# Squaring before clamping in the first activation of an attention and two-MoE kernel

## The chip, the cores and the metric

The kernel runs on one core of a Trainium2 chip. The metric is the device time of one execution in microseconds. Before the change three runs gave 772.76, 773.0 and 776.55 us, a median of 773.0 us.

## The reference

Three stages follow one another over 2304 tokens. The first is attention over a window of 64 keys (4 sequences of 576 tokens, 8 heads of 64). The second is a dense feed-forward layer whose activation is the one changed here:

```python
h = x @ w_in                       # 512 -> 2048
neg, pos = h <= -1, h >= 1
g = np.where(pos, h, np.where(neg, 0.0, (h + 1) ** 2 / 4))
x = g @ w_out                      # 2048 -> 512
```

The third is a mixture of 8 experts, one expert per token, chosen by the largest of 8 gate logits:

```python
idx = argmax(x @ w_gate, axis=1)
out[t] = gate_w[t] * (relu(x[t] @ w1[idx[t]]) @ w2[idx[t]])
```

The inputs are float32. The activation can be written in two ways. For h at most 1, r^2 is at most 1 and max(h, 1) is 1, so both give r^2. For h above 1 the parabola lies above the line h, so both give h.

## The kernel before, in words

Every float32 operand of a matmul is split into a rounded high part and a low part, and a product is made of three passes (high by high, low by high, high by low), all in fp32r.

Tokens are cut into seven blocks of 256 or 384 columns (`BLOCKS`). The second stage goes through steps, one for each block and each of 16 slices of 128 hidden units, 112 steps in all. In a step, `layer1` (L440) makes `h`, 128 hidden units by 256 or 384 tokens, in one of two PSUM buffers with 12 matmuls. `act_g` (L447 to L458) turns `h` into `g`, again in a high and a low part (`ghi`, `glo`). `layer2` (L475) multiplies `g` with `w_out` and adds into `acc`. The main loop issues layer 1 of step i and then layer 2 of step i - 2, so a step's activation has some two steps of matmuls to get done. Layer 1 of step i + 2 needs the PSUM buffer that the activation of step i reads.

`act_g` is a chain over two engines. ScalarE makes `a` = Relu(0.5 h + 0.5) (L449). VectorE clamps it to 1 (L450). ScalarE squares it (L451). VectorE takes the maximum with `h` (L452), which is the last read of `h`. ScalarE rounds the result to `ghi` (L455), and VectorE, or GpSimd for six of the first steps (`GLO_P`), makes `glo` by subtraction (L456). The third stage has a shorter chain, `act_relu` (L464 on ScalarE, L465 on VectorE).

Other work is laid between these steps by slots, two per step. Attention units for later blocks bring score matmuls, a row maximum on VectorE (L336 or L354), exponentials on ScalarE (L364), transposes on TensorE (L399), a copy of them to SBUF as `pb` on ScalarE (L401) and the product with the values (L414). Weight pieces of the second stage are split on ScalarE, VectorE and GpSimd (L180 to L206). From the last block on, VectorE computes the gate logits, one instruction for each of 18 tiles of 128 tokens and each of 8 experts (L569, 144 in all). One expert's weights are then loaded and split (L642 on ScalarE, L643 on GpSimd), and tokens are turned into columns (L160, L910 on ScalarE, L911 on GpSimd). Tokens that didn't choose this expert are gathered at the end.

The order of instructions on each engine isn't the program's order. The program is built under a context that schedules by a simulated timeline, and only the first eight steps have the order of the DMA queue SP written out. So an instruction can run earlier than the place where the program issues it.

```python
with _tile.TileContext(nc, schedule_with_timeline_sim=True) as tc:
    tile_window_attention__then__two_moe_kernel(tc, *args)
```

Of the kernel before, what the change touches and what calls it, by code (L numbers as in the profile page):

```python
# [16 lines left out]
ALU = mybir.AluOpType  # L17
# [93 lines left out]
def kernel(  # L111
# [14 lines left out]
    nc = tc.nc  # L126
# [320 lines left out]
    def act_g(h, n, pool):  # L447
        a = gp.tile([P, NG], F32, tag="a", name="a", bufs=2)
        nc.scalar.activation(a[:, :n], h[:, :n], ACTF.Relu, scale=0.5, bias=half[:, 0:1])  # L449
        nc.vector.tensor_scalar(out=a[:, :n], in0=a[:, :n], scalar1=1.0, scalar2=None, op0=ALU.min)  # L450
        nc.scalar.activation(a[:, :n], a[:, :n], ACTF.Square)  # L451
        nc.vector.tensor_tensor(out=a[:, :n], in0=h[:, :n], in1=a[:, :n], op=ALU.max)  # L452
        hi = gp.tile([P, NG], F32R, tag="ghi", name="ghi")
        lo = gp.tile([P, NG], F32R, tag="glo", name="glo")
        nc.scalar.activation(hi[:, :n], a[:, :n], ACTF.Copy)  # L455
        (nc.gpsimd if pool else nc.vector).tensor_tensor(  # L456
            out=lo[:, :n], in0=a[:, :n], in1=hi[:, :n].bitcast(F32), op=ALU.subtract
        )  # L458
        return hi, lo
# [530 lines left out]
    for i in range(len(steps) + 2):  # L990
        if i == SPN:
            sp_order.close()
        if i < len(steps):
            ph, b, f = steps[i][:3]
            if ph == 1:
                n = blocks[b][1]
                while f not in win:
                    wsplit()
                g[i] = act_g(layer1(xT[b], win[f], n), n, i in GLO_P)
            else:  # L1000
                g[i] = act_relu(layer1(xT2[b], W2["p"][0][f], NG), NG)
        run_slot(base + 2 * i)
        wsplit(base + 2 * i)
        if i >= 2:
            ph, b, f, first, last, partial = steps[i - 2]
            n = blocks[b][1] if ph == 1 else NG
# [93 lines left out]
```

## Time and profile before

| what | value |
|---|---|
| median of three runs | 773.0 us |
| profiled execution | 774.57 us |
| its span | 772.8 us |
| TensorE busy | 727.8 us (94%) |
| VectorE busy | 519.5 us (67%) |
| ScalarE busy | 417.3 us (54%) |
| GpSimd busy | 207.3 us (27%) |

The profile is taken from one execution. Its span reaches from the first to the last instruction; 1.8 us of the execution lie around it. PE is TensorE, DVE is VectorE, ACT is ScalarE, POOL is GpSimd. PEclk is the granted clock of TensorE as a share of 2.4 GHz, so 0.50 stands for 1.2 GHz. A wait is the time that an engine stood idle ahead of an instruction, put down to what released it last.

### The profile page before, as it was taken

The page shows a single profiled execution, that of the slowest core. Times are in us where ns is not written, and L with a number is a line of the kernel's source. Part 1 is how long each engine was busy: PE and PEld are TensorE (multiplying, and loading weights), DVE is VectorE, ACT ScalarE, POOL GpSimd, SP SyncE. Part 2 cuts the span into 40 slices and gives each one's busy share as a digit, 9 for nine tenths or more (in the row PEclk, how much of TensorE's full clock was granted, in tenths as well). Part 3 has the DMA queues.
Part 4 walks back from the last instruction along what each step waited for, and adds up shares of the span by engine and source line. Part 5 has one row for each costly group of instructions (what it writes and reads, how often), then busy time and mean ns, then how long its engine had stood idle before and what let it go on. Part 6 is the DMA issues. An engine that isn't in the chain of part 4 may idle for free. (4 is left out here: it accounts for less than half of the span.)

```text
span 772.8 us, 12584 instructions
## 1 busy us (share of the span) xinstructions
PE 727.8 (94%) x4507; PEld 635.4 (82%) x4507; DVE 519.5 (67%) x1163; ACT 417.3 (54%) x1031; POOL 207.3 (27%) x164
## 2 busy tenths in 40 slices
PE   6698999999999999999999999979999999899996
PEld 3587878888888899888988898768988988799885
DVE  5887988548777668865797398999979854111110
ACT  4777766576656767575677444555533335441212
POOL 2466643204421024300320001561220116520000
PEclk7599999999999999999999999999999999999999
DMA  8446830143432324532343314432353134510101
GB/s 322 158 144 211 281 117 27 56 143 102 146 108 91 117 62 121 152 90 76 82 157 83 149 28 136 145 115 55 127 86 99 33 99 121 155 35 14 42 1 52
DMA packets 66691, 83.78 MB, mean 108 GB/s; under 512 B 35671, under 2 KB 41559, under 8 KB 66498
## 3 DMA queue, kind: packets, MB, share of 16 engines
q1 hardware_dynamic: 66466, 82.52, 34.6%
q8 instruction: 36, 0.59, 0.3%
q0 software_dynamic: 160, 0.43, 0.2%
q14 instruction: 29, 0.24, 0.1%
HBM read 60.74 MB, written 14.42 MB: 97 GB/s over the span
## 5 line engine op out<-in xcount | busy, mean ns | idle before, releaser
L440 PE MATMUL h<-xT,wi 128*128 128x384 f32 (+1 forms) x1344 | 233.5, 322 | 15.8 <-DVE a L452 12.8
L440 PEld LDWEIGHTS h<-xT,wi 128*128 128x128 f32 x1344 | 211.4, 193 | 30.3 <-DVE a L452 21.3
L475 PE MATMUL acc<-wo,ghi 128*128 128x512 f32 x576 | 155.7, 398 | 0.3 <-ACT ghi L455 0.2
L475 PEld LDWEIGHTS acc<-wo,ghi 128*128 128x128 f32 x576 | 104.3, 190 | 16.7 <-ACT ghi L455 1.0
L569 DVE CUSTOM_DVE_ANT_0 junk<-xg,wgb 128x512 bf16<-128x512 f32 x144 | 113.9, 791 | 2.4 <-DMA xg<-x2s 0.6
L440 PE MATMUL h<-xT,we 128*128 128x384 f32 x576 | 110.9, 337 | 3.2 <-DVE glo L465 3.2
L440 PEld LDWEIGHTS h<-xT,we 128*128 128x128 f32 x576 | 102.0, 188 | 9.0 <-DVE glo L465 4.7
L465 DVE SCALAR_TENSOR_TENSOR glo<-h,ghi 128x384 fp32r<-128x384 f32 x48 | 26.6, 554 | 93.2 <-ACT ghi L464 93.2
L475 PE MATMUL acc<-wo,glo 128*128 128x512 f32 x288 | 85.9, 395 | 0.6 <-DVE glo L456 0.5
L475 PE MATMUL acc<-we,ghi 128*128 128x512 f32 x288 | 79.3, 395 | 2.3 <-ACT ghi L464 2.2
L451 ACT ACTIVATE a<-a 128x384 f32<-128x384 f32 (+1 forms) x112 | 53.0, 474 | 50.6 <-DVE a L450 50.3
L456 DVE TENSOR_TENSOR glo<-a,ghi 128x384 fp32r<-128x384 f32 (+1 forms) x106 | 64.8, 612 | 21.4 <-ACT ghi L455 20.6
L455 ACT ACTIVATE ghi<-a 128x384 fp32r<-128x384 f32 (+1 forms) x112 | 53.0, 475 | 42.9 <-DVE a L452 42.0
L449 ACT ACTIVATE a<-h,half 128x384 f32<-128x384 f32 (+1 forms) x112 | 58.8, 525 | 30.5 <-PE h L440 29.1
L452 DVE TENSOR_TENSOR a<-h,a 128x384 f32<-128x384 f32 (+1 forms) x112 | 55.5, 497 | 26.1 <-ACT a L451 25.1
L450 DVE TENSOR_SCALAR a<-a 128x384 f32<-128x384 f32 (+1 forms) x112 | 48.9, 437 | 26.3 <-ACT a L449 26.1
L475 PEld LDWEIGHTS acc<-wo,glo 128*128 128x128 f32 x288 | 53.2, 188 | 13.5 <-DVE glo L456 1.9
L464 ACT ACTIVATE ghi<-h 128x384 fp32r<-128x384 f32 x48 | 23.1, 484 | 75.6 <-PE h L440 63.1
L475 PEld LDWEIGHTS acc<-we,ghi 128*128 128x128 f32 x288 | 52.8, 188 | 10.9 <-ACT ghi L464 2.4
L264 POOL TENSOR_TENSOR qs<-qk,qs 64x512 fp32r<-64x512 f32 x16 | 21.8, 1364 | 132.7 <-ACT qs L257 99.7
L911 POOL TENSOR_TENSOR xT<-xj,xT 128x256 fp32r<-128x256 f32 x36 | 30.5, 855 | 86.8 <-ACT xT L910 86.8
L643 POOL TENSOR_TENSOR we<-er,we 128x512 fp32r<-128x512 f32 x16 | 24.1, 1515 | 95.3 <-ACT we L642 95.3
(170 smaller groups left out, 979.8 us busy)
## 6 DMA issues: line engine op xcount, KB each, us to landing
qk<-in_qk_dram SPq DMA_DIRECT2D x21, 640.0 KB, 3.9
vt<-in_vv_dram SPq DMA_DIRECT2D x32, 256.0 KB, 2.8
er<-in_w_dram SPq DMA_DIRECT2D x32, 256.0 KB, 2.9
wraw<-in_wi_dram SPq DMA_DIRECT2D x14, 512.0 KB, 4.5
wraw<-in_wo_dram SPq DMA_DIRECT2D x14, 512.0 KB, 6.0
xg<-x2s SPq DMA_DIRECT2D x18, 256.0 KB, 2.7
out_dram<-y SPq DMA_DIRECT2D x18, 256.0 KB, 2.3
qk<-in_qq_dram SPq DMA_DIRECT2D x11, 320.0 KB, 3.2
```

Source lines behind the costliest of these rows:

```text
L440: nc.tensor.matmul(h[:, :n], w[:, wa, k * P:k * P + P], x[:, xa, k, :n], start=(i == 0), stop=(i == 3 * KD - 1),)
L449: nc.scalar.activation(a[:, :n], h[:, :n], ACTF.Relu, scale=0.5, bias=half[:, 0:1])
L450: nc.vector.tensor_scalar(out=a[:, :n], in0=a[:, :n], scalar1=1.0, scalar2=None, op0=ALU.min)
L451: nc.scalar.activation(a[:, :n], a[:, :n], ACTF.Square)
L452: nc.vector.tensor_tensor(out=a[:, :n], in0=h[:, :n], in1=a[:, :n], op=ALU.max)
L455: nc.scalar.activation(hi[:, :n], a[:, :n], ACTF.Copy)
L456: (nc.gpsimd if pool else nc.vector).tensor_tensor(out=lo[:, :n], in0=a[:, :n], in1=hi[:, :n].bitcast(F32), op=ALU.subtract)
L465: nc.vector.scalar_tensor_tensor(out=lo[:, :n], in0=h[:, :n], scalar=0.0, in1=hi[:, :n].bitcast(F32), op0=ALU.max, op1=ALU.subtract,)
L475: nc.tensor.matmul(a, ga[:, t * P:t * P + P], w[:, wa], start=(first and j == 0), stop=(last and j == 2),)
L569: nc.vector.tensor_tensor_reduce(out=junk, in0=xg[t], in1=Z["wgb"][:, e], scale=1.0, scalar=0.0, op0=ALU.mult, op1=ALU.add, accum_out=Z["L ...
L643: nc.gpsimd.tensor_tensor(out=w[:, 1], in0=raw, in1=w[:, 0].bitcast(F32), op=ALU.subtract)
L911: (nc.vector if 2 * t + i in PL_V else nc.gpsimd).tensor_tensor(out=lo, in0=r, in1=hi.bitcast(F32), op=ALU.subtract)
```

## The change

The clamp of L450 is gone. ScalarE does Relu and Square one after the other. One VectorE instruction then computes max(h, 1) and takes the minimum of that and the square, in a single pass with two operations.

```diff
     def act_g(h, n, pool):
         a = gp.tile([P, NG], F32, tag="a", name="a", bufs=2)
         nc.scalar.activation(a[:, :n], h[:, :n], ACTF.Relu, scale=0.5, bias=half[:, 0:1])
-        nc.vector.tensor_scalar(out=a[:, :n], in0=a[:, :n], scalar1=1.0, scalar2=None, op0=ALU.min)
         nc.scalar.activation(a[:, :n], a[:, :n], ACTF.Square)
-        nc.vector.tensor_tensor(out=a[:, :n], in0=h[:, :n], in1=a[:, :n], op=ALU.max)
+
+        nc.vector.scalar_tensor_tensor(
+            out=a[:, :n], in0=h[:, :n], scalar=1.0, in1=a[:, :n], op0=ALU.max, op1=ALU.min
+        )
```

## Rows read from the trace of the kernel before

**Rows 1.** The page's first part: busy us, share of the span, instructions.
```profile
PE 727.8 (94%) x4507; PEld 635.4 (82%) x4507; DVE 519.5 (67%) x1163; ACT 417.3 (54%) x1031; POOL 207.3 (27%) x164
```

**Rows 2.** Waits of PE, 80:478 then 478:546: total us, times, longest.
```profile
PE h L440 <- DVE a L452: 4.0, 9, 0.8
...
PE h L440 <- DVE a L452: 8.8, 5, 4.1
```

**Rows 3.** Busy us of PE, PEld, DVE, ACT, POOL by stretch; clock; DMA share; GB/s.
```profile
80.00:478.00 398.00, 391.01 (x2530) 343.42 (x2523) 294.86 (x619) 248.61 (x634) 91.78 (x59) 1.00 0.36 110
478.00:546.00 68.00, 59.18 (x277) 52.14 (x276) 66.95 (x156) 38.07 (x75) 31.62 (x24) 0.95 0.36 106
```

**Rows 4.** Groups of VectorE by form: busy us, mean ns, idle before, releaser.
```profile
L452 DVE TENSOR_TENSOR a<-h,a 128x384 f32<-128x384 f32 x64 | 35.3, 554 | 12.5 <-ACT a L451 12.1
...
L465 DVE SCALAR_TENSOR_TENSOR glo<-h,ghi 128x384 fp32r<-128x384 f32 x48 | 26.6, 554 | 93.2 <-ACT ghi L464 93.2
```

**Rows 5.** Tile `a`: ns min/median/max, first and last start; who waited for it.
```profile
L450 DVE TENSOR_SCALAR a<-a x112: 266/350/1698, 40.1 to 540.9; 128x384 f32<-128x384 f32 x64, 128x256 f32<-128x256 f32 x48
...
L452 DVE TENSOR_TENSOR a<-h,a x112: 393/546/559, 41.5 to 543.1; 128x384 f32<-128x384 f32 x64, 128x256 f32<-128x256 f32 x48
...
  ACT a L451: 50.3, 57
```

**Rows 6.** Timeline of ScalarE: start us, us, instruction, [idle before it <- releaser].
```profile
438.93 0.53 ACT L451 ACTIVATE a<-a 128x384 f32<-128x384 f32 x1 [0.43 <-DVE a L450]
...
505.28 0.79 ACT L160 ACTIVATE xj<-tt 128x512 uint16<-128x512 uint16 x1 [2.20 <-DVE glo L456]
506.11 0.42 ACT L910 ACTIVATE xT<-xj 128x256 fp32r<-128x256 f32 x1
```

**Rows 7.** Timeline of TensorE around 63 us.
```profile
62.16 0.66 PE L399 MATMUL pt<-ct,sr 128*128 128x128 f32 x4
64.88 1.46 PE L414 MATMUL av<-pb,vt 128*64 128x64 f32 x16 [2.07 <-ACT pb L401]
```

**Rows 8.** Timeline of ScalarE around 64 us.
```profile
63.92 0.42 ACT L451 ACTIVATE a<-a 128x256 f32<-128x256 f32 x1 [1.86 <-DVE a L450]
64.25 0.58 ACT L401 ACTIVATE pb<-pt 128x512 f32<-128x512 f32 x1
```

**Rows 9.** The stretch behind that wait, columns as in rows 3.
```profile
65.10:68.40 3.30, 3.30 (x23) 2.99 (x22) 2.04 (x5) 3.23 (x14) 2.42 (x2) 0.50 0.54 174
```

**Rows 10.** Timeline of VectorE around 178 us.
```profile
177.45 1.37 DVE L450 TENSOR_SCALAR a<-a 128x256 f32<-128x256 f32 x1
179.30 0.43 DVE L452 TENSOR_TENSOR a<-h,a 128x256 f32<-128x256 f32 x1 [0.48 <-ACT a L451]
```

**Rows 11.** Timeline of TensorE at 180 us.
```profile
179.78 1.70 PE L440 MATMUL h<-xT,wi 128*128 128x256 f32 x12 [0.49 <-DVE a L452]
```

**Rows 12.** Busy us of L450 alone, then of L569 alone; clock; DMA; GB/s.
```profile
479.00:523.00 44.00, 4.06 (x8) 0.96 0.42 124
...
478.00:546.00 68.00, 45.95 (x99) 0.95 0.36 106
```

**Rows 13.** Timeline of VectorE: the first gate logit, and one at 520 us.
```profile
444.80 0.69 DVE L569 CUSTOM_DVE_ANT_0 junk<-xg,wgb 128x512 bf16<-128x512 f32 x1 [0.58 <-DMA xg<-x2s]
...
519.75 1.75 DVE L569 CUSTOM_DVE_ANT_0 junk<-xg,wgb 128x512 bf16<-128x512 f32 x1
```

**Rows 14.** Timeline of TensorE in the last block.
```profile
464.91 2.35 PE L440 MATMUL h<-xT,wi 128*128 128x384 f32 x12
...
497.70 2.38 PE L440 MATMUL h<-xT,wi 128*128 128x384 f32 x12 [1.57 <-DVE a L452]
...
508.41 3.89 PE L440 MATMUL h<-xT,wi 128*128 128x384 f32 x12 [2.05 <-DVE a L452]
...
522.77 3.76 PE L440 MATMUL h<-xT,wi 128*128 128x384 f32 x12 [4.06 <-DVE a L452]
```

**Rows 15.** Timeline of GpSimd at 520 us.
```profile
519.58 1.38 POOL L643 TENSOR_TENSOR we<-er,we 128x512 fp32r<-128x512 f32 x1
```

## Prediction

> **What bounds the kernel now.** I read the page's first part, then the waits of TensorE, then the table of stretches, then the timelines around the waits it names. The page gives TensorE 727.8 of 772.8 us and VectorE 519.5 [rows 1]: matmuls are the bound and VectorE has room on average. An average hides the stages, so TensorE's waits are asked for by stage. From 80 to 478 us, where attention and the first layers run interleaved, it waits nine times for L452, 4.0 us in all; from 478 to 546 us five times, 8.8 us in all [rows 2]. L452 is the last reader of `h`, and `h` has two PSUM buffers, so layer 1 two steps later can't start before it. The two stages differ: in the first VectorE is busy 294.86 of 398 us, in the second 66.95 of 68 [rows 3]. In the first L452 is late because of latency and queueing, in the second because VectorE itself is the bound. There its work is the gate logits of L569, 45.95 us of the 68 [rows 12].
>
> **What the change removes.** The 112 VectorE instructions of L450, with a median of 350 ns and up to 1698 ns [rows 5]. And two crossings between engines: ScalarE waited 57 times, 50.3 us, for L450 before its Square [rows 5]. Where nothing queues that wait is 0.43 us [rows 6]. Afterwards Square follows Relu on the same engine. How soon a dependent ScalarE instruction starts is seen at 505.28 plus 0.79, which ends at 506.07; the one that reads its output starts at 506.11 [rows 6], so 0.04 us. An undisturbed chain gains 0.43 - 0.04 = 0.4 us.
>
> **What it adds.** L452 becomes a scalar_tensor_tensor with the same inputs, `h` in PSUM and `a`. Its nearest row is L465, the same form with a PSUM and an SBUF input: 554 ns at 384 columns, and the old L452 takes 554 too [rows 4]. I take no difference. Bounds: 350 ns below (L450's median, if it ran like that form), and above 554 + 350 = 904, both old instructions in one; even that would be no more VectorE time than now. It waits for Square, and what stands behind it on VectorE (mask adds, the row maxima, the weight splitting, gate logits) waits too. Before, that queue waited in two pieces, for Relu and for Square; now in one.
>
> What a change of order does I can't see. The code asks for scheduling by a simulated timeline, and the trace shows the reach of that: the first gate logit runs at 444.80 [rows 13], while the program issues it behind the first layer-1 group of the last block, which TensorE reaches at 464.91 [rows 14]. So a freed place on VectorE can be refilled with a gate logit from later. All three terms below carry this doubt.
>
> **Term A, the wait at 62.8 us.** The transposes end at 62.16 + 0.66 = 62.82, and the next matmuls start at 64.88 after 2.07 us of waiting for `pb` [rows 7]. ScalarE made `pb` late: it stood 1.86 us at Square, waiting for L450, and only then did the `pb` copy at 64.25, 0.58 us [rows 8]. Without L450 ScalarE is free by 62.5, the copy starts when the transposes end, about 62.85, and ends at 63.43; TensorE starts about 63.5. That is 64.88 - 63.48 = 1.4 us; what is late next is the copy itself. Right behind this wait the granted clock is 0.50, the 1.2 GHz level, for 3.3 us [rows 9]. The price of such a stretch is seen at 508.41: twelve matmuls take 3.89 us, at 497.70 the same twelve take 2.38 [rows 14], so 1.5 us. The wait of 1.57 us at 497.70 was followed by no such fall, so I count it as gone. A = 2.9 us; bounds 0 and 3.6 (2.07 + 1.5).
>
> **Term C, the nine waits from 80 to 478 us.** The one at 179.78 [rows 11] is typical of those that go whole: L450 took 1.37 us where its median is 0.35, and ended at 178.82, Square followed, L452 started at 179.30 [rows 10]. With Square done long before, the one VectorE instruction starts at 177.45 and ends before 178. Where L452 stands behind other VectorE work, only L450's own place, 0.35 us, comes back. The nine make 4.0 us; bounds 0 and 4.0. I take 2.4, six tenths.
>
> **Term E, VectorE bound from 478 to 546 us.** Between 479 and 523 us eight L450 take 4.06 us [rows 12], and the waits grow to 1.57, 2.05 and 4.06 us [rows 14]. If nothing refills the places, the last of these comes 4.1 us sooner. If gate logits refill them all, only the shorter chain is left, 0.4 to 0.7 us, since `h` comes free that much earlier once. I take 2.0, near the middle. Two of these waits are followed by matmuls at half the clock, 508.41 and 522.77 [rows 14]; I leave both as they are, and keep 2 x 1.5 us as a bound.
>
> **Sum.** 2.9 + 2.4 + 2.0 = 7.3 us. New waits from a new order I take at nothing, with 3.6 us (the largest wait of this kind and its half clock, as in A) either way. The profiled execution took 774.57 us (span 772.8 and 1.8 around it), so 767.3 for it. The median of the runs, 773.0, lies 1.6 below that execution: 765.7 us.
>
> **Rivals.**
> 1. More: the places on VectorE stay free, all three half-clock stretches go and the nine waits too: 2.9 + 4.0 + 4.1 + 3.0 = 14.0 us, 759.0. For it: all of them hang on L452 or L450. Against it: the gate logits run ahead of their place already, so VectorE refills.
> 2. Nothing that counts: ScalarE and VectorE work in order, and 62.8 us or 179.8 us only shows which instruction was ahead. In a new order another stands there, and A and C turn into waits of the same size. Left is E: 773.0 - 2.0 = 771.0. For it: 4.0 us of wait in 398 us is little, and any order leaves something. Against it: the 50.3 us that ScalarE waited for L450 [rows 5] go whatever the order.
> 3. Slower: the refill on the VectorE-bound stretch puts one more gate logit ahead of each of the eight instructions up to 523 us. While GpSimd works, such a logit is stretched: the one at 519.75 took 1.75 us, beside an L643 from 519.58, where the one at 444.80 took 0.69 [rows 13, 15]. Eight times 1.75 is 14.0, less the 4.06 of L450, plus one more half-clock stretch, 1.5, is 11.4 slower; A and C gain 5.3, so 6.1 is left and 779.1. It decides from 8x = 4.06 + 5.3, a mean of 1.2 us per extra logit; the mean of the stage is 45.95 over some 49 logits [rows 12], 0.94, so they would have to fall on GpSimd's work. For it: VectorE is full there [rows 3]. Against it: there is less work on VectorE for the same steps. The Trainium skill, GPSIMD Engine Reference, section Specifications, has a rule that bears on it: GpSimd contends with VectorE instructions that have two SBUF inputs or run in a two-port mode. A gate logit has two SBUF inputs, L452 has one in PSUM, and the trace agrees: L452 never took more than 559 ns [rows 5]. By that rule the extra logits cost 1.75 each and the time is 779.1; without it they would cost 0.69, 5.5 less 4.06 is 1.4, and the time would be 773.0 - 5.3 + 1.4 = 769.1.
> 4. The change doesn't do what it says, if the order puts other ScalarE work between Relu and Square and `h` is held as long as before: 773.
>
> **How the numbers follow.** Forecast 0.46, its own range 762 to 769; rival 1 0.14; rival 2 0.26; rival 3 0.12; rival 4 0.02. A measurement here tells about 0.5%, 3.9 us, from no change: below 769.1 is faster, above 776.9 slower. Faster: 0.45 + 0.14 + 0.04 of rival 2 = 0.63; slower: 0.10 of rival 3 and 0.01 of rival 2's far end; the rest, 0.26, is the same. The range of 8 in 10 runs from 758.5, just beyond rival 1, to 773.5: rival 2 with 2.5 us of new waits. It leaves out rival 3 and the ends of 1 and 2.
>
> **What would show it.** L450 is gone from the groups, VectorE's busy time falls by at least 112 x 0.35 = 39 us, and the new instruction takes 554 ns at 384 columns and is never stretched. ScalarE's wait of 50.3 us goes; its wait for L452's successor before L455 stays. A is right if TensorE waits under 1 us for `pb` near 63 us and the clock stays at 1.00 there. C is right if the waits for the successor of L452 between 80 and 478 us sum to under 2 us. E is right if the 8.8 us of the later stage fall to about 6 to 7, with as many gate logits before 546 us as now or a few more. It is wrong if that stage's waits grow, or if waits of TensorE for other releasers appear between 40 and 478 us in the place of those that went.

## The result, and the profile after

The changed kernel takes 763.86 us, the median of four runs (763.68 to 765.28); the kernel before, beside it, 773.31 (772.76 to 776.55). The ratio is 0.9856, with a 95% interval of 0.9832 to 0.988. The profiled execution took 765.28 us with a span of 763.5. Lines from L452 on have moved: L452 is now the single VectorE instruction, L450 is Square, L457 and L458 make `ghi` and `glo`, L467 is the old L465, L477 the old L475 and L571 the old L569.

First the page's first part, as in [rows 1]:

```profile
PE 722.4 (95%) x4507; PEld 633.2 (83%) x4507; DVE 469.9 (62%) x1051; ACT 418.2 (55%) x1031; POOL 207.9 (27%) x164
```

VectorE lost 112 instructions and 49.6 us. The groups by form answer to [rows 4], the page of tile `a` (durations, then who waited: us, times) to [rows 5]:

```profile
L452 DVE SCALAR_TENSOR_TENSOR a<-h,a 128x384 f32<-128x384 f32 x64 | 35.4, 554 | 30.1 <-ACT a L450 29.7
```

```profile
L450 ACT ACTIVATE a<-a x112: 399/507/542, 41.2 to 530.3; 128x384 f32<-128x384 f32 x64, 128x256 f32<-128x256 f32 x48
L452 DVE SCALAR_TENSOR_TENSOR a<-h,a x112: 409/547/559, 41.8 to 532.1; 128x384 f32<-128x384 f32 x64, 128x256 f32<-128x256 f32 x48
...
  DVE a L452: 52.7, 48
  ACT ghi L457: 48.0, 63
```

The new instruction costs 554 ns at 384 columns, as the old one did, and its longest is 559. ScalarE's 50.3 us of waiting ahead of Square have no row any more.

The two stretches of [rows 3], then TensorE's waits in each, as in [rows 2] (total us, times, longest):

```profile
80.00:478.00 398.00, 396.52 (x2562) 352.42 (x2560) 265.51 (x551) 255.04 (x644) 93.72 (x61) 1.00 0.38 113
478.00:546.00 68.00, 60.25 (x287) 52.33 (x286) 67.24 (x155) 37.02 (x75) 32.26 (x25) 0.97 0.36 105
```

```profile
PE S L297 <- DMA qk<-in_qq_dram: 0.9, 1, 0.9
PE S L315 <- DVE sr L324: 0.3, 1, 0.3
```

```profile
PE h L440 <- DVE a L452: 6.3, 6, 2.2
PE h L440 <- DVE glo L467: 1.1, 1, 1.1
PE acc L477 <- DVE glo L458: 0.4, 1, 0.4
```

From 80 to 478 us none of the nine waits for L452 is left. In the last block VectorE is as full as before, and L452 still makes TensorE wait.

To see where the time came from, read off in both traces when the first matmul of a step's layer 1 starts, and subtract. The table does so for every kernel run here; what each is comes below. Times are us of the profiled execution. The last two columns are TensorE's waits for `h` and `g` in the last block (from step 96 to step 112) and the number of stretches there, of about 3.4 us each, with a granted clock of 0.50.

| kernel | to step 12 | 12 to 96 | 96 to 112 | from 112 | waits in 96 to 112 | half-clock |
|---|---|---|---|---|---|---|
| before | 97.3 | 363.4 | 80.3 | 231.8 | 8.8 | 2 |
| before, again | 98.1 | 363.1 | 80.2 | 230.6 | 9.5 | 1 |
| after | 98.4 | 354.0 | 77.1 | 234.0 | 6.7 | 1 |
| after, again | 100.5 | 354.2 | 77.5 | 233.9 | 7.0 | 1 |
| s1 | 98.2 | 362.5 | 81.2 | 227.7 | 9.8 | 1, twice as long |
| s2 | 98.0 | 353.2 | 78.5 | 234.6 | 9.1 | 0 |
| s3 | 98.9 | 363.2 | 80.9 | 228.9 | 9.1 | 2 |
| s5 | 97.5 | 353.7 | 78.2 | 230.7 | 8.9 | 0 |
| x1 | 97.7 | 355.7 | 79.8 | 232.4 | 9.3 | 1 |
| x2 | 99.0 | 360.0 | 78.9 | 235.1 | 8.7 | 1 |
| x3 | 97.2 | 353.7 | 77.0 | 240.7 | 6.0 | 2 |
| x4 | 98.4 | 353.8 | 70.6 | 239.7 | 1.8 | 0 |
| c1 | 98.4 | 354.2 | 72.3 | 231.7 | 2.8 | 1 |

The change gained 9.4 us from step 12 to 96 and 3.2 in the last block, and lost 1.1 ahead of them and 2.1 behind.

The 9.4 us are more than the 4.0 us of waits that went, and more than the 4.9 us by which TensorE's waits of every kind fell from 80 to 478 us (6.1 to 1.2). The rows of the weight loads (PEld) say why. At 151.7 us in the kernel before, one wait stands in both (start us, us, instruction, idle before it):

```profile
151.74 0.74 PE L440 MATMUL h<-xT,wi 128*128 128x256 f32 x4 [0.50 <-DVE a L452]
...
151.73 0.65 PEld L440 LDWEIGHTS h<-xT,wi 128*128 128x128 f32 x5 [0.94 <-DVE a L452]
```

The matmul ahead of it started at 150.84. Where nothing waits the next one starts 0.23 us later; here 0.90, so 0.67 us were lost and the matmul row shows 0.50 of them. The ends of matmuls are modelled in the profile, and short waits disappear in them. Waits of the weight load from 97 to 460 us, of before, then of after:

```profile
PEld h L440 <- DVE a L452: 9.6, 16, 1.3
...
PEld acc L475 <- DVE glo L456: 1.9, 3, 0.8
...
PEld acc L475 <- ACT ghi L455: 0.5, 2, 0.3
```

```profile
PEld h L440 <- DVE a L452: 0.3, 1, 0.3
```

These 12.0 us overstate it, as 0.94 overstates 0.67. The starts of the matmuls themselves settle it: over the 84 steps the first matmul of layer 1 starts 21.3 us (summed) behind the matmul ahead of it before, and 15.4 after, which is 6.0 us. The layer-2 matmuls, each against the median distance of such a pair, come 2.8 us earlier. The rest is 0.6.

The chain itself got shorter by 0.9 us in the mean: over these 84 steps it takes 3.16 us from Relu's start to the end of L452 before, and 2.23 after. Most of that lay between Relu's end and Square's start, 1.33 us before and 0.29 after. Where nothing queues, the old clamp starts 0.03 us after Relu's end and Square 0.03 us after the clamp's, so the way between the engines is short and the chain's loss was the clamp itself and its place in VectorE's queue.

### The profile page after: what moved, and what is told of

Its sections match the earlier page's. It is cut to its first block, busy times and chain, and to the rows that moved or that the text cites. A ratio compares the mean times of both kernels' runs of the same rounds, so it can differ in the third digit from the quotient of the medians.

```text
span 763.5 us, 12427 instructions
## 1 busy us (share of the span) xinstructions
PE 722.4 (95%) x4507; PEld 633.2 (83%) x4507; DVE 469.9 (62%) x1051; ACT 418.2 (55%) x1031; POOL 207.9 (27%) x164
## 5 line engine op out<-in xcount | busy, mean ns | idle before, releaser
L440 PE MATMUL h<-xT,wi 128*128 128x384 f32 (+1 forms) x1344 | 230.5, 318 | 8.0 <-DVE a L452 6.3
L477 PE MATMUL acc<-wo,ghi 128*128 128x512 f32 x576 | 155.4, 398 | 2.0 <-ACT ghi L457 1.1
L477 PEld LDWEIGHTS acc<-wo,ghi 128*128 128x128 f32 x576 | 103.7, 189 | 17.8 <-ACT ghi L457 1.5
L571 DVE CUSTOM_DVE_ANT_0 junk<-xg,wgb 128x512 bf16<-128x512 f32 x144 | 115.6, 803 | 2.8 <-DMA xg<-x2s 0.5
L452 DVE SCALAR_TENSOR_TENSOR a<-h,a 128x384 f32<-128x384 f32 (+1 forms) x112 | 55.5, 497 | 53.5 <-ACT a L450 52.7
L477 PE MATMUL acc<-wo,glo 128*128 128x512 f32 x288 | 86.2, 396 | 0.4 <-DVE glo L458 0.4
L467 DVE SCALAR_TENSOR_TENSOR glo<-h,ghi 128x384 fp32r<-128x384 f32 x48 | 26.6, 555 | 96.7 <-ACT ghi L466 96.5
L458 DVE TENSOR_TENSOR glo<-a,ghi 128x384 fp32r<-128x384 f32 (+1 forms) x106 | 68.3, 644 | 27.4 <-ACT ghi L457 27.3
L477 PE MATMUL acc<-we,ghi 128*128 128x512 f32 x288 | 79.2, 395 | 2.4 <-ACT ghi L466 2.2
L457 ACT ACTIVATE ghi<-a 128x384 fp32r<-128x384 f32 (+1 forms) x112 | 53.0, 475 | 48.4 <-DVE a L452 48.0
L477 PEld LDWEIGHTS acc<-wo,glo 128*128 128x128 f32 x288 | 53.8, 189 | 13.5 <-DVE glo L458 0.8
L477 PEld LDWEIGHTS acc<-we,ghi 128*128 128x128 f32 x288 | 52.8, 188 | 10.8 <-ACT ghi L466 2.4
L450 ACT ACTIVATE a<-a 128x384 f32<-128x384 f32 (+1 forms) x112 | 52.9, 475 | 2.2
L264 POOL TENSOR_TENSOR qs<-qk,qs 64x512 fp32r<-64x512 f32 x16 | 21.4, 1340 | 109.4 <-ACT qs L257 80.9
L913 POOL TENSOR_TENSOR xT<-xj,xT 128x256 fp32r<-128x256 f32 x36 | 29.4, 821 | 80.3 <-ACT xT L912 80.3
L267 POOL TENSOR_TENSOR qs<-qk,qs 128x768 fp32r<-128x768 f32 x18 | 34.9, 1940 | 59.2 <-DVE qs L259 36.0
```

Of the source, the lines that this page charges most:

```text
L267: keng.tensor_tensor(out=k, in0=raw[:, 512:], in1=kh.bitcast(F32), op=ALU.subtract)
L440: nc.tensor.matmul(h[:, :n], w[:, wa, k * P:k * P + P], x[:, xa, k, :n], start=(i == 0), stop=(i == 3 * KD - 1),)
L452: nc.vector.scalar_tensor_tensor(out=a[:, :n], in0=h[:, :n], scalar=1.0, in1=a[:, :n], op0=ALU.max, op1=ALU.min)
L458: (nc.gpsimd if pool else nc.vector).tensor_tensor(out=lo[:, :n], in0=a[:, :n], in1=hi[:, :n].bitcast(F32), op=ALU.subtract)
L467: nc.vector.scalar_tensor_tensor(out=lo[:, :n], in0=h[:, :n], scalar=0.0, in1=hi[:, :n].bitcast(F32), op0=ALU.max, op1=ALU.subtract,)
L477: nc.tensor.matmul(a, ga[:, t * P:t * P + P], w[:, wa], start=(first and j == 0), stop=(last and j == 2),)
```

## The experiments

Two theories stood against each other. L: the gain is local, it arises where the new form is used, since `h` and `g` come free sooner. O: the scheduler happened on a better order as a whole, and the gain would come with any such edit. The first four kernels choose the form by step, with the same function:

```diff
-    def act_g(h, n, pool):
+    def act_g(h, n, pool, new):
...
+        if new:
+            nc.scalar.activation(a[:, :n], a[:, :n], ACTF.Square)
+            nc.vector.scalar_tensor_tensor(
...
+        else:
+            nc.vector.tensor_scalar(out=a[:, :n], in0=a[:, :n], scalar1=1.0, scalar2=None, op0=ALU.min)
...
-                g[i] = act_g(layer1(xT[b], win[f], n), n, i in GLO_P)
+                g[i] = act_g(layer1(xT[b], win[f], n), n, i in GLO_P, i < 12)
```

**s1, the new form in the first 12 steps alone.**

> The new form in steps 0 to 11 only (up to about 97 us), the old one in the other 100. Theory L (each stage gains what shortening the chain gives there, and the stages add up): between the traces of before and after this stage lost some 0.7 us (the first layer-1 group of step 12 came at 97.27 before and at 98.40 after, and the first step started 0.48 us later), so about 0.7 us slower than before, ratio 1.000 to 1.002. Theory O (the gain is luck of one new order, any edit reshuffles the whole program): a change of several us of either sign in the stages that keep the old form, ratio anywhere from 0.992 to 1.008.

773.32 us, ratio 0.9976 (0.9955 to 0.9996). Up to step 12 it is 0.9 us longer, from there to 96 0.9 shorter: the 9.4 don't come. The 4.1 us that it gains behind step 112, in a stage that was not edited, L did not expect.

**s2, the new form in steps 12 to 95 alone** (`12 <= i < 96`).

> The new form in steps 12 to 95 only. Theory L: this is where after gained against before (9.4 us between the starts of steps 12 and 96), so 764 to 766, ratio 0.988 to 0.991, and the nine waits of 4.0 us of TensorE for L452 between 80 and 478 us go as they went in after. Theory O: no part of the gain need come back; ratio 0.992 to 1.004, with waits of TensorE left between 80 and 478 us.

765.14 us, ratio 0.9876 (0.9852 to 0.9901). The stage gains 10.2 us. L stands.

**s3, the new form from step 96 alone** (`i >= 96`).

> The new form in the last block only (steps 96 to 111), where VectorE is full. Theory L: between the traces that block and what follows gained about 1.0 us (3.2 in the block, 2.2 given back behind it), so 771 to 773, ratio 0.997 to 1.000, the waits for L452 in the block fall from 8.8 us to about 6. The prediction's rival of a costly refill: more gate logits ahead of the block's steps and a longer block, ratio over 1.003. Theory O: anything between 0.993 and 1.007.

775.36 us, ratio 1.0017 (1.0001 to 1.0033), slower than L expected. The stage of steps 12 to 96 keeps its 363 us. The last block does not gain alone: its waits stay at 9.1 us, both stretches at half the clock remain, and 61 gate logits start within it where 58 did before.

**s5, the new form below step 96** (`i < 96`).

> The new form in steps 0 to 95 and the old one in the last block. If the stages add up (the runs so far: steps 0 to 11 alone 0.9976, steps 12 to 95 alone 0.9876, the last block alone 1.0017): 0.985 to 0.986, the same as after or a little faster, 763 to 764. If the last block needs the new form (the waits there were 9.1 us with the old form and 6.3 with the new): 765 to 768, ratio 0.988 to 0.991.

763.96 us, ratio 0.9859 (0.9835 to 0.9882), the same as the changed kernel. In the last block the old form waits 2.2 us longer than the new (8.9 against 6.7), but no stretch at half the clock follows, and the block takes 78.2 us instead of 77.1.

So L holds for steps 12 to 96: 353.2 to 354.2 us with the new form there, in every kernel that has it without further work in the chain, and 362.5 to 363.4 with the old. Behind step 112 it is O that holds. None of the four edits touches that stage, and it takes from 227.7 to 234.6 us in them.

The next two ask what the 9.4 us are made of: VectorE's smaller work, or the chain without the crossing from ScalarE to VectorE and back. **x1** gives VectorE nearly the old clamp's work back beside the chain (256 or 368 columns), on a constant, into a tile that is overwritten:

```diff
+        nc.vector.tensor_scalar(
+            out=hi[:, :k], in0=ct[:, :k], scalar1=1.0, scalar2=None, op0=ALU.min
+        )
         nc.vector.scalar_tensor_tensor(
```

> The kernel after, with VectorE's old work put back beside the chain: per step one tensor_scalar of 256 or 368 columns from the constant tile, which nothing in the chain from h to a waits for (its output is overwritten by ghi). If the gain is the shorter chain (theory L), most of it stays: 764 to 767, ratio 0.988 to 0.993. If the gain is VectorE's saved time (112 instructions, about 49 us), it goes: 770 to 774, ratio 0.996 to 1.001. In the last block, where VectorE is full, both expect the waits for the chain's VectorE instruction to come back to about 8.8 us.

768.58 us, ratio 0.9929 (0.9901 to 0.9956), between the two ranges. From step 12 to 96 7.7 of the 9.4 us stay. In the last block the waits are back at 9.3 us, as was expected either way.

**x2** keeps the crossing and hardly any work, one column of VectorE between Relu and Square:

```diff
+        nc.vector.tensor_scalar(out=a[:, :1], in0=a[:, :1], scalar1=0.0, scalar2=None, op0=ALU.max)
         nc.scalar.activation(a[:, :n], a[:, :n], ACTF.Square)
```

> The kernel after, with the two crossings put back and the work left out: between Relu and Square a VectorE instruction on one column of a (the maximum with 0, which changes nothing), so ScalarE waits for VectorE's queue again. Theory L (the gain before the last block is the shorter chain): the gain between steps 12 and 96, 9.4 us, goes for the larger part, TensorE's weight loads wait for L452's successor between 97 and 460 us for 5 us or more again (9.6 before, 0.3 after); 769 to 773, ratio 0.994 to 0.999. If VectorE's saved time were the gain: 764 to 767, ratio 0.988 to 0.992.

772.53 us, ratio 0.9963 (0.9945 to 0.9982). From step 12 to 96 only 3.4 of 9.4 us are left, and the waits return under the old reader and under the column (weight load, 97 to 460 us):

```profile
PEld h L440 <- DVE a L452: 2.8, 2, 1.6
...
PEld h L440 <- DVE a L450: 2.2, 1, 2.2
```

So with the crossing alone back 5.9 us are lost, and with the work alone back 1.6. The other 1.8 are lost only with both. The chain of x2 takes 2.93 us in the mean, with 1.02 between Relu and Square, though the column takes 0.15; that of x1 takes 2.52.

These aren't the sixteen waits of before: they are three long ones at other places. In each of them Square was done, and L452 stood behind other VectorE instructions that came between the column and it; it started 2.4, 1.3 and 2.7 us after Square's end. (The third is put down to the column, that of a later step, since it ended last.) At the first, the end of Square on ScalarE, then VectorE:

```profile
193.59 0.40 ACT L451 ACTIVATE a<-a 128x256 f32<-128x256 f32 x1
...
194.25 2.23 DVE L520 COPY pl<-prow 128x1024 uint16<-128x1024 uint16 x1
196.40 0.41 DVE L452 SCALAR_TENSOR_TENSOR a<-h,a 128x256 f32<-128x256 f32 x1
```

A crossing thus costs as a second place in a full queue. How much of the 5.9 us is that, and how much is x2's own order, one kernel can't tell.

Three kernels look at the last block, all built on the changed kernel. **c1** leaves out GpSimd's 16 subtractions for the expert's weights; ScalarE writes zeros in their place:

```diff
-        nc.gpsimd.tensor_tensor(out=w[:, 1], in0=raw, in1=w[:, 0].bitcast(F32), op=ALU.subtract)
+        if name == "we":
+            nc.scalar.activation(w[:, 1], raw, ACTF.Copy, scale=0.0)
+        else:
+            nc.gpsimd.tensor_tensor(out=w[:, 1], in0=raw, in1=w[:, 0].bitcast(F32), op=ALU.subtract)
```

> The kernel after, where the low parts of the chosen expert's weights are left out: ScalarE writes zeros in their place (16 activations), and GpSimd's 16 subtractions of some 1.6 us in the last block are gone. If the last block's waits come from GpSimd stretching VectorE's instructions there (gate logits of up to 1.8 us): the logits stay near 0.7 us, the waits for L452 in the block fall from 6.3 us to under 2, no matmul there runs at half the clock, 756 to 760, ratio 0.978 to 0.983. If the number of logits is what fills VectorE: the waits stay over 4 us, 762 to 765, ratio 0.985 to 0.990.

758.24 us, ratio 0.9778 (0.9747 to 0.9808). Groups of VectorE from 460 to 540 us, first of the changed kernel, then of c1 (busy us, mean ns):

```profile
L571 DVE CUSTOM_DVE_ANT_0 junk<-xg,wgb 128x512 bf16<-128x512 f32 x61 | 55.8, 915 | 0.7
L458 DVE TENSOR_TENSOR glo<-a,ghi 128x384 fp32r<-128x384 f32 x15 | 12.0, 798 | 0.0
L452 DVE SCALAR_TENSOR_TENSOR a<-h,a 128x384 f32<-128x384 f32 x15 | 8.3, 551 | 1.7 <-ACT a L450 1.7
```

```profile
L571 DVE CUSTOM_DVE_ANT_0 junk<-xg,wgb 128x512 bf16<-128x512 f32 x69 | 50.9, 738 | 0.9
L458 DVE TENSOR_TENSOR glo<-a,ghi 128x384 fp32r<-128x384 f32 x15 | 9.1, 609 | 0.8 <-ACT ghi L457 0.6
L452 DVE SCALAR_TENSOR_TENSOR a<-h,a 128x384 f32<-128x384 f32 x15 | 8.3, 552 | 4.7 <-ACT a L450 4.7
```

With GpSimd quieter (9.9 us busy in this window where it was 35.3) the logits and `glo` are shorter, L452 is not, and the waits fall from 6.7 to 2.8 us. The last block is bound by VectorE work that GpSimd stretches. One stretch at half the clock stays, which was not expected.

**x4** lets those subtractions come later, with one buffer `er` for the raw weights in place of two; **x3** slows the logits' supply of rows in the same way (`xg`).

```diff
-        raw = Z["p2"].tile([P, 512], F32, tag="er", name="er", bufs=2)
+        raw = Z["p2"].tile([P, 512], F32, tag="er", name="er", bufs=1)
```

> The kernel after with one buffer instead of two for the raw pieces of the expert weights, so that a piece is loaded only when GpSimd has split the one before, and GpSimd's 16 subtractions spread from 474 to 521 us over a longer stretch. Theory L with GpSimd's stretching as the cause of the last block's waits: fewer gate logits are stretched ahead of the block's steps, the waits for L452 there fall from 6.3 us to 2 to 5, and the pieces still come in time for the third stage; 759 to 763, ratio 0.981 to 0.986. Rival: the same stretching falls on later logits and the third stage waits for VectorE or for its weights; 764 to 770, ratio 0.987 to 0.995.

765.07 us, ratio 0.9871 (0.9849 to 0.9892). The last block falls to 70.6 us and the third stage gives 5.7 of its 6.5 us back, the rival of the expectation. TensorE's waits from 540 us on, and ScalarE at one of their sources:

```profile
PE h L440 <- DVE glo L467: 6.8, 8, 1.9
```

```profile
540.20 0.63 ACT L644 ACTIVATE we<-er 128x512 fp32r<-128x512 f32 x1 [2.05 <-DMA er<-in_w_dram]
540.74 0.47 ACT L466 ACTIVATE ghi<-h 128x384 fp32r<-128x384 f32 x1
```

The weight split waits for its DMA at the head of ScalarE's queue, and `ghi` of the third stage stands behind it.

> The kernel after with one buffer instead of two for the token rows of the gate logits (and for the gathered rows at the end), so that the eight logits of a tile wait for their load and fewer of them stand ahead of the last block's steps. If the waits of the last block (8.9 us of weight loads, 6.3 of matmuls) come from the logits that stand ahead in VectorE's queue: they fall by 3 us or more and the time to 758 to 762, ratio 0.980 to 0.986, as long as the logits still end before the tail needs them. If they come from GpSimd slowing whatever VectorE does there: no change beyond 2 us, 762 to 766, ratio 0.985 to 0.991. A third way: the choice of the expert comes later and its weights arrive late at the third stage, over 768.

770.04 us, ratio 0.992 (0.9893 to 0.9947). The block takes 77.0 us as before the edit, and the logits fall into the third stage, the last of them at 628 us where it was 596, with 8.8 us of waits from 540 us on:

```profile
PE h L440 <- DVE glo L467: 8.8, 8, 3.6
```

Last, both kernels unchanged, a second execution each.

> The changed kernel as it is, a second execution. It prices the stages' scatter. If the differences of 1 us up to step 12 and of 2 to 4 us behind step 112 belong to the kernels, this run repeats the first one's: -1.1 us up to step 12, +9.4 from 12 to 96, +3.2 from 96 to 112 and -2.1 behind it, each within 0.4, against the kernel before. If they are scatter between executions, the first and the last of these move by 1 us and by 2 to 4 us, while the instructions and their order stay the same, and the 9.4 stays within 0.5.

> The kernel before as it is, a second execution. If the stages' small differences belong to the kernels, every stage repeats within 0.4 us (97.3 us to step 12, 363.4 from 12 to 96, 80.3 from 96 to 112, 231.8 behind it). If they are scatter, the first moves by up to 1.6 us and the last by 2 to 4, and the nine waits for L452 from 80 to 478 us return with the same sum, 4.0 us, within 1.

767.77 us and 773.76 us, one run each. The 9.4 comes again as 9.0 (354.2 and 363.1 us), and the last blocks repeat (77.5 and 80.2). The first 97 us don't: 100.5 against 98.4 us for the same program, 98.1 against 97.3. The stage from step 112 keeps its difference: 233.9 us against 230.6. So the loss there, 2 to 3 us, isn't scatter; it belongs to the changed kernel's order, and s5 shows that an order with the new form below step 96 can be without it (230.7).

## Why the prediction was right, and where it was not

The forecast, 765.7 us and faster, held to 1.8 us, and that closeness is luck. By the table term C came out 7.0 us larger than forecast and E 1.2, A 4.0 smaller, and 2.1 were lost behind step 112 where nothing was counted; these nearly cancel. The direction is no luck: the gain of C is shown by s2, s5 and what s1 and s3 lack.

**The prices held.** The new instruction was taken at the old one's 554 ns and took them; VectorE's busy time fell by 49.6 us where at least 39 were asked for.

**Term A failed.** The wait at 62.8 us is gone, but rival 2's mechanism put others in its place (TensorE, 50 to 73 us):

```profile
50.56 0.97 PE L414 MATMUL av<-pb,vt 128*64 128x64 f32 x16 [1.47 <-ACT pb L401]
...
65.08 1.20 PE L477 MATMUL acc<-wo,ghi 128*128 128x512 f32 x4 [1.12 <-ACT ghi L457]
...
73.00 1.13 PE L477 MATMUL acc<-wo,ghi 128*128 128x512 f32 x2 [0.83 <-ACT wo L205]
```

The stretch at half the clock moved too, from 65 to 73 us:

```profile
73.10:76.50 3.40, 3.40 (x10) 2.52 (x11) 1.78 (x5) 3.37 (x14) 2.87 (x3) 0.50 0.94 322
```

2.9 us were forecast; 1.1 was lost. Of that loss nothing is shown, since the same program scatters by 2.1 us in this stage. Over all kernels of the table the stage takes 97.2 to 100.5 us with the new form in it and 97.3 to 98.9 with the old, so no gain is seen there. What failed is the step that says "what is late next is the copy itself": it looked at one place of an order that the scheduler made anew.

**Term C was right in kind and mis-sized.** All nine waits went, where the forecast asked for under 2 us of them to be left. But 2.4 us were forecast with 4.0 as the upper bound, and 9.4 came. The failing step is "the nine make 4.0 us; bounds 0 and 4.0": it took the matmul row for the whole loss. The weight loads showed 16 waits of 9.6 us for the same reader, and layer 2's waits for `ghi` and `glo`, worth 2.8 us, weren't in the sum. The discount to six tenths, for L452 standing behind other work, was wrong as well. In eight of the sixteen it started within 0.04 us of Square's end, in the other eight it came 0.17 to 2.48 us after it, behind other VectorE work; both kinds went. The term also took the clamp's 0.35 us for all that comes back in a queue, where the chain got 0.9 us shorter in the mean.

**Term E came out in size, and its reason is not shown.** 8.8 us of waits were to become 6 to 7; they became 6.7, and the block got 3.2 us shorter where 2.0 were forecast. But s3, with the clamp gone in this block alone, keeps waits of 9.1 us with three gate logits more, the case of the refill; and s2 and s5, with the old form in it, have a block 1.8 and 2.1 us shorter than before. The waits fell only where the new form stood in the block and in the steps before it, and x1, with the work put back, has them at 9.3. Why both are needed stays open. One of the two stretches at half the clock went besides, which the sum had as a bound; the kernel before has only one in its second execution, so that can't be laid to the change. Behind this wait the other one stayed:

```profile
510.09 3.88 PE L440 MATMUL h<-xT,wi 128*128 128x384 f32 x12 [2.20 <-DVE a L452]
```

s5 shows how little the new form in this block is worth by itself: with the old one the waits are 2.2 us longer, but the clock falls behind none of them, the third stage is 3.3 us shorter, and the kernel's time is the same.

**New waits from a new order, taken at 0 with 3.6 either way, cost 2 to 3 us** behind step 112. They are waits for `glo` of the third stage, 5.1 us instead of 3.2:

```profile
541.29 1.83 PE L440 MATMUL h<-xT,we 128*128 128x384 f32 x9 [1.09 <-DVE glo L467]
556.88 2.37 PE L440 MATMUL h<-xT,we 128*128 128x384 f32 x12 [0.69 <-DVE glo L467]
...
578.69 1.85 PE L440 MATMUL h<-xT,we 128*128 128x384 f32 x9 [1.72 <-DVE glo L467]
```

This is rival 3's refill in another place. Counted in the traces, 81 gate logits run ahead of the first L467 and five between it and the second; before, 77 and four. That this order makes the whole loss isn't shown: s1 has the same counts as before, 77 and four, and takes 4.1 us less than it, so something else counts too, and what it is stays open. In the last block itself there was no refill: between its first and last step 59 logits start, 58 before.

Rival 3's price rested on GpSimd stretching the logits, and c1 measures it: 915 ns against 738 for a logit, 798 against 609 for `glo`, 551 against 552 for L452. The Trainium skill, GPSIMD Engine Reference, section Specifications, has GpSimd contend with VectorE instructions that read two SBUF inputs; these rows agree, for L452 reads `h` from PSUM.

## What to carry to other kernels

Price a wait of TensorE from the starts of its matmuls, or from the weight-load row as an upper bound, and ask who else waits for the same chain further on; the idle time ahead of a matmul can show much less than was lost, here 3.8 us of 6.0. In a chain that goes back and forth between two engines, count the places that it takes in a full engine's queue: here a second place for an instruction of 0.15 us cost 5.9 us in one kernel, the old instruction's work beside the chain 1.6. Take terms that rest on one place of a scheduled order as worth nothing when the scheduler runs again, and test a gain in a full stage together with the stage behind it.

## What the runs showed of the hardware

The last block adds up over all thirteen executions: its length is 69.2 us, plus TensorE's waits in it, plus 1.1 us for each stretch of about 3.4 us at a granted clock of 0.50 (1.2 GHz), within 0.8 us (s1's long stretch counts as two; 69.2 and 1.1 are fitted to these thirteen). So the block's length doesn't go by its waits alone. Nor does the wait's length alone tell whether the clock falls: first s5, whose last reader of `h` is L458, then c1, at the same step after the same wait.

```profile
504.49 2.37 PE L440 MATMUL h<-xT,wi 128*128 128x384 f32 x12 [1.98 <-DVE a L458]
```

```profile
502.33 3.23 PE L440 MATMUL h<-xT,wi 128*128 128x384 f32 x12 [1.98 <-DVE a L452]
```

The same instructions take 2.37 us in the one and 3.23 in the other, where the clock fell within them. And the same program's first 97 us differed by 2.1 us between two executions, with TensorE's waits for L297's first DMAs at 5.0 us in the second against 3.3, and the matmuls behind the later of them starting at 11.89 us against 10.59, while its stage of 354 us repeated within 0.2.
